# Attention with mixed heads and a PReLU layer: rows of a group 12 or 9 partitions apart, and two fixed places for side work in each block

## The chip, the cores and the metric

The kernel runs on one core of a Trainium2 chip. The metric is the device time of one execution in microseconds (us), taken as the median of several runs. Engines are named as the profile names them: PE is TensorE's matmul stream and PEld its weight loads, DVE is VectorE, ACT is ScalarE, POOL is GpSimd, SP is SyncE, which here only starts DMAs. All arithmetic on the activations of the first half is fp32.

## The reference

B = 4, H = 12 heads, S = 448, D = 64; the second half has DM = 768 and DFF = 2048.

```python
scores = q @ k.T / sqrt(D)                       # per head
scores = einsum('bhij,hg->bgij', scores, w_pre)  # heads mixed
attn = softmax(scores, axis=-1)
attn = einsum('bhij,hg->bgij', attn, w_post)     # mixed again
x = (attn @ v) laid out as (B*S, H*D)
h = x @ w_in
out = (max(h, 0) + alpha * min(h, 0)) @ w_out
```

## The kernel before, in words

The program has two halves. The first (to about 545 us) does the attention, and beside it VectorE turns the float64 weights of the second half into fp32. The second half (from about 553 us) is a stream of matmuls. The change touches the first half alone.

**Chunks and groups.** The 448 query rows of a batch are cut into chunks of 110, 110, 110 and 118 rows (L27). For a chunk and one head pair `qk` (L140) puts raw scores into a PSUM tile `s`, and ScalarE copies them into the SBUF tile `st` (L155), which holds one query row per partition, with 12 heads times 448 keys behind it. Head mixing needs the 12 heads of a row on 12 partitions. So a chunk is cut into groups of GI = 10 rows, and `relay` (L159) moves a group with one SBUF-to-SBUF DMA, from 10 partitions of `st` to the 120 partitions of a tile `sr`. There are 180 groups, 45 in a batch, and two of them make a block: 90 blocks. Each relay moves 10 x 12 pieces of 448 floats (1,792 bytes), 215,040 bytes in all. There are eight `sr` buffers, so relays run up to four blocks ahead.

**A block.** `mix` multiplies the two relayed groups by the weights into PSUM tile `m` (L170, 8 matmuls); VectorE takes the negated row maxima `nm` (L175); ScalarE takes two exponentials into `e` (L182), one for each half u; `norm` makes the scaled second mixing weights `r`; two blocks later `post` does the second mixing, transposing as it goes, into the one PSUM tile `pa` (L204, 56 matmuls), and ScalarE copies `pa` in two pieces into `at` (L214).

**Side work.** For each chunk there are six `qk` jobs (8 matmuls and one eviction by ScalarE each), and two `pv` jobs, which multiply `at` by `v` (L226, 84 matmuls) and are evicted by a ScalarE copy (L235), a VectorE addition (L236) and a DMA to the DRAM tensor `x2` (L237). The PSUM tiles of both kinds, `s` and `x`, share one buffer (`ps_s`, one tile of two banks), so that a job's matmuls wait for the eviction of the job before it.

**What sets the order.** Each engine works through its own instructions in program order, and `step(m)` writes that order: the mix of block m+1, the DMAs left over from the step before, the relays of block m+4, norm and maximum, both exponentials of block m, the first side job with its eviction, the second mixing of block m-2 with its copies, then all other side jobs with theirs. A table `jobs` says which side jobs fall into which step. Relays are issued by SP for even groups and by POOL for odd ones (the first eight by SP, ACT and POOL).

Of the kernel before, what the change touches and what calls it, by code (L numbers as in the profile page):

```python
# [14 lines left out]
ALU = mybir.AluOpType  # L15
# [7 lines left out]
GI = 10  # L23
GP = GI * H
HI = GI // 2
HP = HI * H
CHUNKS = [(0, 110), (110, 110), (220, 110), (330, 118)]  # L27
CW = 118
NCC = DM // 128
NFC = DFF // 128  # L30
NP = H // 2
NS = 4
NJ = S // 64
SR0 = 4
RAHEAD = 3
LAG = 2
# [24 lines left out]
def talking_heads_prelu(ctx: ExitStack, tc: tile.TileContext, q, k, v, w_pre, w_post, mask, w_in, w_out, alpha, out):  # L61
    nc = tc.nc
# [2 lines left out]

    groups, first = [], []
    chunk_list = [(b, c) for b in range(B) for c in range(len(CHUNKS))]
    for ci, (b, c) in enumerate(chunk_list):  # L70
        first.append(len(groups))
        cn = CHUNKS[c][1]
        for r in range(0, cn, GI):
            groups.append((ci, min(r, cn - GI)))
    NG, NC = len(groups), len(chunk_list)
    NB = NG // 2
    first.append(NG)
# [34 lines left out]
    k_t, q_t, v_t, s_t, a_t = {}, {}, {}, {}, {}  # L112
# [8 lines left out]

    def load_q(ci, dmas=None):
        b, c = chunk_list[ci]
        c0, cn = CHUNKS[c]
        q_t[ci] = qp.tile([128, NP, CW], F32, tag="q", name=f"q{ci}")
        for hf in range(2):
            dma = dmas[hf] if dmas else nc.gpsimd
            dma.dma_start(out=q_t[ci][64 * hf:64 * hf + 64, :, :cn],
                          in_=q[b, :, H * c0 + NP * hf * cn:H * c0 + NP * (hf + 1) * cn])
# [7 lines left out]
    u_t = {}  # L137

    def qk(ci, p, ps_pool=None):
        b, c = chunk_list[ci]  # L140
        cn = CHUNKS[c][1]
        ps = (ps_pool or ps_s).tile([128, 2, 512], F32, tag="m" if ps_pool else "s", name=f"s{ci}_{p}")
# [7 lines left out]
    def qk_out(ci, p, copy=nc.scalar.copy):  # L150
        cn = CHUNKS[chunk_list[ci][1]][1]
        if p == 0:
            s_t[ci] = sp.tile([CW, H, S], F32, tag="s", name=f"st{ci}")
        dst = s_t[ci].rearrange("p (t n) s -> p n t s", t=2)
        copy(dst[:cn, p], u_t.pop(("qk", ci, p))[:cn, :, :S])  # L155

    sr_t, m_t, nm_t, e_t, se_t, r_t = {}, {}, {}, {}, {}, {}

    def relay(n, dma):  # L159
        ci, r = groups[n]  # L160
        sr_t[n] = sr_b[n % NSR]
        dma.dma_start(out=sr_t[n][SR0:SR0 + GP], in_=s_t[ci][r:r + GI])  # L162

    def mix(m):

# [7 lines left out]
    def rmax(m):  # L173
        nm = sm.tile([128, 2], F32, tag="nm", name=f"nm{m}")
        nc.vector.tensor_reduce(out=nm, in_=m_t[m][:, :, :S], axis=AX.X, op=ALU.max, negate=True)  # L175
        nm_t[m] = nm

    def exp(m, u):
        if u == 0:
            e_t[m] = ep.tile([128, 2, S], F32, tag="e", name=f"e{m}")  # L180
            se_t[m] = sm.tile([128, 2], F32, tag="se", name=f"se{m}")
        nc.scalar.activation(out=e_t[m][:, u], in_=m_t[m][:, u, :S], func=AF.Exp, bias=nm_t[m][:, u:u + 1], scale=1.0,  # L182
                             accum_out=se_t[m][:, u:u + 1])
# [12 lines left out]
    def post(m):  # L196
        e, r = e_t.pop(m), r_t.pop(m)
        for u in range(2):
            for jb in range(NJ):
                s, c = divmod(jb, 2)  # L200
                for g in range(2):
                    h = slice(64 * g, 64 * g + 64)
                    dst = pa[64 * c:64 * c + 64, g, s * GP:(s + 1) * GP].rearrange("p (h i) -> p h i", h=H)
                    nc.tensor.matmul(dst[:, :, HI * u:HI * u + HI], e[h, u, 64 * jb:64 * jb + 64],  # L204
                                     r[h, u].rearrange("p (h i) -> p h i", h=H), start=True, stop=True)

    def post_out(m):
        for g in range(2):
            n = 2 * m + g
            ci, r = groups[n]  # L210
            if n == first[ci]:
                a_t[ci] = ap_.tile([128, NS, H, CW], F32, tag="a", name=f"at{ci}")
            dst = a_t[ci].rearrange("p s h i -> p (s h) i")[:, :, r:r + GI]
            nc.scalar.copy(dst, pa[:, g, :NS * GP].rearrange("p (s i) -> p s i", i=GI))  # L214

    def pv(ci, hx, ps_pool=None):
        b, c = chunk_list[ci]
        cn = CHUNKS[c][1]
        ps = (ps_pool or ps_s).tile([128, 2, 512], F32, tag="m" if ps_pool else "s", name=f"x{ci}_{hx}")
        for cl in range(3):  # L220
            for s in range(NS):
                for t in range(2):
                    h = 2 * (3 * hx + cl) + t
                    for r in range(2 if 2 * s + 1 < NJ else 1):
                        pr = slice(64 * r, 64 * r + 64)
                        nc.tensor.matmul(ps[64 * t:64 * t + 64, r, cl * CW:cl * CW + cn], v_t[b][pr, s, h * D:(h + 1) * D],  # L226
                                         a_t[ci][pr, s, h, :cn], start=(s == 0), stop=(2 * s + 2 + r >= NJ))
        u_t["pv", ci, hx] = ps

    def pv_out(ci, hx):  # L230
        b, c = chunk_list[ci]
        c0, cn = CHUNKS[c]
        xe = xep.tile([128, 3, CW], F32, tag="xe", name=f"xe{ci}_{hx}")
        src = u_t.pop(("pv", ci, hx))[:, :, :3 * CW].rearrange("p r (c i) -> p r c i", c=3)
        nc.scalar.copy(xe[:, :, :cn], src[:, 0, :, :cn])  # L235
        nc.vector.tensor_tensor(xe[:, :, :cn], src[:, 1, :, :cn], xe[:, :, :cn], ALU.add)  # L236
        later.append(lambda: nc.sync.dma_start(  # L237
            out=x2[3 * hx:3 * hx + 3, :, b * S + c0:b * S + c0 + cn].rearrange("c p i -> p c i"), in_=xe[:, :, :cn]))

# [27 lines left out]
    jobs = {}  # L267

    def at(m, f, *args):
        jobs.setdefault(m, []).append((f, args))  # L270

    for ci, (b, c) in enumerate(chunk_list):
        if ci:
            m0, m1 = first[ci - 1] // 2 - RAHEAD, first[ci] // 2 - RAHEAD - 2
            for p in range(NP):
                at(max(m0 + p * (m1 - m0) // (NP - 1), p // 2), "qk", ci, p)
        if ci >= 2:
            at(max(first[ci - 2] // 2 - 1, 0), "load", load_q, ci)
        if c == 0:
            if b:  # L280
                at(first[ci] // 2 - 15, "load", load_k, b)
            at(first[ci] // 2 + 3 if b else 1, "load", load_v, b)
        lb = (first[ci + 1] - 1) // 2
        at(lb + LAG + 1, "pv", ci, 0)
        at(lb + LAG + (3 if ci + 1 < NC else 1), "pv", ci, 1)
    conv_steps = NFC * 2 * 7

    with tc.manual_schedule():
# [24 lines left out]
        for i, w in enumerate((w_pre, w_post)):  # L313
            for p in ((SR0, 64), (0, 64))[i]:
                nc.gpsimd.dma_start(out=mask_sb[p:p + HP, i], in_=mask[:HP, :HI, :])
                nc.gpsimd.dma_start(out=wb[p:p + HP, i, :],
                                    in_=w.rearrange("(o h) g -> o h g", o=1).to_broadcast([HI, H, H]))
# [5 lines left out]
            out=wk[:, :HP].rearrange("p (i g) -> p i g", g=H), in0=mask_sb[:, 0], scalar=scale,  # L323
# [4 lines left out]
            out=wq.rearrange("p g i -> p i g"), in0=mask_sb[:, 1],  # L328
# [9 lines left out]
        def relays(upto, dmas):  # L338
            nonlocal relayed
            while relayed < min(upto, NG):  # L340
                relay(relayed, dmas[relayed % len(dmas)])
                relayed += 1

        relays(2 * (RAHEAD + 1), (nc.sync, nc.scalar, nc.gpsimd))
        done = 0
        live = lambda m: 0 <= m < NB
        EV = {"qk": (qk, qk_out), "pv": (pv, pv_out)}

        def step(m):
            nonlocal done  # L350
            todo = jobs.get(m, [])
            for f, args in todo:
                if f == "load":
                    args[0](*args[1:])
            uses = [(f, args) for f, args in todo if f != "load"]
            if live(m + 1):
                mix(m + 1)
            now, later[:] = list(later), []
            for f in now:
                f()  # L360
            if m >= 0:
                relays(2 * (m + 2 + RAHEAD) if m > 2 else first[1], (nc.sync, nc.gpsimd))
            if live(m - 1):
                norm(m - 1)
            if live(m + 1):
                rmax(m + 1)
            if live(m):
                exp(m, 0)
                exp(m, 1)
            for f, args in uses[:1]:  # L370
                EV[f][0](*args)
                EV[f][1](*args)
            if live(m - LAG):
                post(m - LAG)
                post_out(m - LAG)
            for f, args in uses[1:]:
                EV[f][0](*args)
                EV[f][1](*args)
            want = (m + 1) * conv_steps // (NB - 4)
            while done < want and done < conv_steps:  # L380
                next(conv, None)
                done += 1
# [95 lines left out]
        for u in range(NU + 1):  # L478
            b, f = divmod(u, NFC)
# [4 lines left out]
            if u < NU:  # L484
                split_w(u, 1)
                ps = l1(u)
# [44 lines left out]
```

## Time and profile before

| what | us |
|---|---|
| median of 3 runs | 1043.7 |
| lowest and highest | 1034.62, 1052.75 |
| the profiled execution | 1041.12 |
| its span | 1038.9 |
| PE busy in the span | 869.1 |
| DVE, ACT, POOL busy | 500.2, 441.6, 348.7 |

Busy shares mix two halves of the program with different limits, so the rows further down are read by stretch. Between the profiled execution and its span lie 2.2 us.

### The profile page before, as it was taken

The numbers are of one execution on the slowest core, as the hardware profiler recorded it, in microseconds if no ns is written. First come the engines' busy times: TensorE is split into PE (matmuls) and PEld (weight loads), VectorE is DVE, ScalarE is ACT, GpSimd is POOL, SyncE is SP. The second block draws the span as 40 slices with busy tenths as digits, with TensorE's granted clock in tenths as the row PEclk, the third lists the DMA queues.
The fourth block names the chain that finished last, engine by engine and source line by source line (L and its number), as shares of the span: only waits on it lengthen the run. The fifth ranks groups of instructions, "written<-read, shape, count | busy, mean of one in ns | idle before, by whom it ended". The sixth has DMA issues, their size and how long they took to land.

```text
span 1038.9 us, 26286 instructions
## 1 busy us (share of the span) xinstructions
PE 869.1 (84%) x11540; PEld 687.8 (66%) x11540; DVE 500.2 (48%) x886; ACT 441.6 (43%) x870; POOL 348.7 (34%) x305
## 2 busy tenths in 40 slices
PE   4656767867868687778666999999999999999998
PEld 2134444544535355455455999999999999999997
DVE  3454666656657376758624224632265224542222
ACT  1453666655657466648342232323233323232322
POOL 3121222222212122211004455554455454545452
PEclk9687898988889798889796999999999999999999
DMA  7698878897899977898618600020001000010001
GB/s 149 154 185 193 173 190 204 220 220 179 167 228 213 200 191 181 186 247 176 145 32 316 271 1 19 1 89 1 1 19 63 27 1 9 9 54 1 1 1 53
DMA packets 55209, 123.86 MB, mean 119 GB/s; under 512 B 21080, under 2 KB 38840, under 8 KB 54712
## 3 DMA queue, kind: packets, MB, share of 16 engines
q0 software_dynamic: 15232, 59.01, 25.7%
q1 hardware_dynamic: 38546, 60.12, 20.7%
q10 hardware_dynamic: 1318, 3.08, 1.2%
q8 instruction: 90, 1.47, 0.6%
q14 instruction: 23, 0.19, 0.1%
HBM read 59.85 MB, written 23.59 MB: 80 GB/s over the span
## 4 chain that ended last, share of the span: by engine, by line
PE 67%; DMA 16%; ACT 7%; issue 5%; DVE 4%; SPq 1%; POOL 0%; ACTq 0%; DVEq 0%; POOLq 0%
PE h L435 23%; PE acc L460 23%; DMA sr<-st 14%; PE s L147 7%; PE x L226 6%; PE m L170 4%; PE pa L204 4%; ACT st L155 3%; ACT at L214 2%; ACT e L182 1%; DMA xr<-x 1%; DMA wb<-in_w_post_dram 1%; DMA cr<-in_w_out_dram 1%; DVE xe L236 1%; DVE nm L175 1%
## 5 line engine op out<-in xcount | busy, mean ns | idle before, releaser
L435 PE MATMUL h<-xs,wi 128*128 128x448 f32 x1152 | 251.4, 371 | 12.6 <-DVE xs L425 11.3
L460 PE MATMUL acc<-g,wo 128*128 128x448 f32 x1152 | 248.2, 368 | 0.0
L435 PEld LDWEIGHTS h<-xs,wi 128*128 128x128 f32 x1152 | 218.4, 190 | 35.4 <-issue 11.5
L460 PEld LDWEIGHTS acc<-g,wo 128*128 128x128 f32 x1152 | 216.2, 188 | 21.8
L413 POOL TENSOR_TENSOR wi<-wr,wi 128x768 fp32r<-128x768 f32 x64 | 118.6, 1853 | 269.8 <-ACT wi L412 269.8
L204 PEld LDWEIGHTS pa<-r,e 64*64 64x64 f32 x5040 | 115.4, 146 | 79.6 <-issue 55.4
L175 DVE TENSOR_REDUCE nm<-m 128x2 f32<-128x896 f32 x90 | 97.9, 1088 | 135.7 <-PE m L170 135.5
L444 DVE TENSOR_SCALAR t<-h,alpha_sb 128x448 f32<-128x448 f32 x64 | 43.8, 684 | 245.7 <-PE h L435 245.7
L204 PE MATMUL pa<-r,e 64*64 64x60 f32 x5040 | 121.9, 234 | 43.6 <-issue 33.8
L170 PE MATMUL m<-sr,wk 64*64 64x448 f32 (+1 forms) x720 | 111.6, 650 | 50.4 <-DMA sr<-st 43.2
L446 ACT CAST g<-t 128x448 fp32r<-128x448 f32 x64 | 36.3, 567 | 275.2 <-DVE t L445 275.2
L162 POOL DMA_DIRECT2D sr<-st x88 | 54.2, 617 | 276.9 <-PE m L170 185.0
L147 PE MATMUL s<-k,q 64*46 64x448 f32 (+2 forms) x768 | 112.7, 640 | 39.5 <-ACT st L155 27.8
L214 ACT COPY at<-pa 128x480 f32<-128x480 f32 x180 | 93.2, 572 | 82.2 <-PE pa L204 82.0
L413 POOL TENSOR_TENSOR wo<-wr,wo 128x768 fp32r<-128x768 f32 x64 | 123.8, 1935 | 7.6 <-ACT wo L412 5.9
L182 ACT ACTIVATE e<-m,nm 128x448 f32<-128x448 f32 x180 | 113.7, 646 | 14.2 <-DVE nm L175 14.2
L226 PEld LDWEIGHTS x<-at,v 64*64 64x64 f32 x2688 | 88.2, 146 | 37.6 <-issue 20.3
L155 ACT COPY st<-s 110x896 f32<-110x896 f32 (+1 forms) x93 | 84.6, 909 | 63.0 <-PE s L147 55.6
L226 PE MATMUL x<-at,v 64*64 64x110 f32 (+1 forms) x2688 | 92.6, 280 | 18.5 <-issue 13.3
L147 PEld LDWEIGHTS s<-k,q 64*64 64x64 f32 (+2 forms) x768 | 27.5, 140 | 92.3 <-ACT st L155 70.9
L170 PEld LDWEIGHTS m<-sr,wk 64*64 64x64 f32 (+1 forms) x720 | 29.3, 151 | 77.5 <-issue 64.7
L412 ACT CAST wo<-wr 128x768 fp32r<-128x768 f32 x64 | 53.8, 841 | 62.3 <-PE acc L460 62.3
(46 smaller groups left out, 564.1 us busy)
## 6 DMA issues: line engine op xcount, KB each, us to landing
sr<-st SPq DMA_DIRECT2D x89, 210.0 KB
sr<-st POOLq DMA_DIRECT2D x88, 210.0 KB, 9.7
cr<-in_w_in_dram POOLq DMA_DIRECT2D x16, 768.0 KB, 11.5
cr<-in_w_out_dram POOLq DMA_DIRECT2D x16, 768.0 KB, 10.1
wsc<-ct SPq DMA_DIRECT2D x32, 384.0 KB
wr<-wsc SPq DMA_DIRECT2D x14, 768.0 KB
xr<-x SPq DMA_DIRECT2D x24, 224.0 KB
out_dram<-o SPq DMA_DIRECT2D x24, 224.0 KB
```

The lines of the kernel that those rows point to most:

```text
L147: nc.tensor.matmul(ps[lo:hi, hf, :S], q_t[ci][r, p, lo:hi], k_t[b][r, p, :], start=True, stop=True)
L155: copy(dst[:cn, p], u_t.pop(("qk", ci, p))[:cn, :, :S])
L162: dma.dma_start(out=sr_t[n][SR0:SR0 + GP], in_=s_t[ci][r:r + GI])
L170: nc.tensor.matmul(ps[hf:hf + 64, u, :S], wk[r, :], g[r, :], start=True, stop=True)
L175: nc.vector.tensor_reduce(out=nm, in_=m_t[m][:, :, :S], axis=AX.X, op=ALU.max, negate=True)
L182: nc.scalar.activation(out=e_t[m][:, u], in_=m_t[m][:, u, :S], func=AF.Exp, bias=nm_t[m][:, u:u + 1], scale=1.0, accum_out=se_t[m][:, u:u ...
L204: nc.tensor.matmul(dst[:, :, HI * u:HI * u + HI], e[h, u, 64 * jb:64 * jb + 64], r[h, u].rearrange("p (h i) -> p h i", h=H), start=True, s ...
L214: nc.scalar.copy(dst, pa[:, g, :NS * GP].rearrange("p (s i) -> p s i", i=GI))
L226: nc.tensor.matmul(ps[64 * t:64 * t + 64, r, cl * CW:cl * CW + cn], v_t[b][pr, s, h * D:(h + 1) * D], a_t[ci][pr, s, h, :cn], start=(s == ...
L413: nc.gpsimd.tensor_tensor(t[:, 1], w, t[:, 0], ALU.subtract)
L435: nc.tensor.matmul(ps[:, :S], w[:, tw, cc * 128:(cc + 1) * 128], x[:, tx, cc, :], start=(i == 0), stop=(i == 3 * NCC - 1))
L460: nc.tensor.matmul(accs[c][:, :S], w[:, tw, c * 128:(c + 1) * 128], g[:, tg], start=(f == 0 and i == 0), stop=(f == NFC - 1 and i == 2))
```

## The change

Chunks become 120, 120, 120 and 97 rows. A new table ROWS gives for each chunk the first row used and the distance between the rows of a group: a group of a 120-row chunk is rows r, r+12, ..., r+108, and there are 12 such groups; in the last chunk a group is rows 7+r, 16+r, ..., 88+r, nine groups that use 90 of its 97 rows (two rows of the sequence are computed twice). The relay thus reads ten partitions 12 or 9 apart where it read ten neighbours; its pieces, its destination and its bytes are the same, and there are still 180 groups and 90 blocks. Since a group's rows are no longer neighbours, `at` keeps groups one behind the other, and the eviction of `pv` puts rows back into order by writing `xe` with a step of 12 or 9 floats.

In `step`, the second mixing now stands ahead of the side jobs, and there are at most two of those in a step. The first one's eviction comes after the copies of the second mixing. The second one's eviction is held over to the next step, where it stands between the two exponentials. Relays are issued behind that held eviction. A new table places the jobs.

```diff
-CHUNKS = [(0, 110), (110, 110), (220, 110), (330, 118)]
-CW = 118
+CHUNKS = [(0, 120), (120, 120), (240, 120), (351, 97)]
+ROWS = [(0, 12), (0, 12), (0, 12), (7, 9)]
+CW = 120
...
-        cn = CHUNKS[c][1]
-        for r in range(0, cn, GI):
-            groups.append((ci, min(r, cn - GI)))
+        for r in range(ROWS[c][1]):
+            groups.append((ci, r))
...
-        dma.dma_start(out=sr_t[n][SR0:SR0 + GP], in_=s_t[ci][r:r + GI])
+        r0, st = ROWS[chunk_list[ci][1]]
+        r0 += r
+        dma.dma_start(out=sr_t[n][SR0:SR0 + GP], in_=s_t[ci][r0:r0 + (GI - 1) * st + 1:st])
...
-            dst = a_t[ci].rearrange("p s h i -> p (s h) i")[:, :, r:r + GI]
+            dst = a_t[ci].rearrange("p s h i -> p (s h) i")[:, :, r * GI:(r + 1) * GI]
...
-        src = u_t.pop(("pv", ci, hx))[:, :, :3 * CW].rearrange("p r (c i) -> p r c i", c=3)
-        nc.scalar.copy(xe[:, :, :cn], src[:, 0, :, :cn])
-        nc.vector.tensor_tensor(xe[:, :, :cn], src[:, 1, :, :cn], xe[:, :, :cn], ALU.add)
+        ps = u_t.pop(("pv", ci, hx))[:, :, :3 * CW].rearrange("p r (c i) -> p r c i", c=3)
+        src = [ps[:, r, :, :cn].rearrange("p c (g i) -> p c g i", i=GI) for r in range(2)]
+        dst = xe[:, :, :cn].rearrange("p c (i g) -> p c g i", i=GI)
+        nc.scalar.copy(dst, src[0])
+        nc.vector.tensor_tensor(dst, src[1], dst, ALU.add)
...
-            uses = [(f, args) for f, args in todo if f != "load"]
+            uses = sorted(((f, args) for f, args in todo if f != "load"), key=lambda u: u[0] != "pv")
             if live(m + 1):
                 mix(m + 1)
...
-            if m >= 0:
-                relays(2 * (m + 2 + RAHEAD) if m > 2 else first[1], (nc.sync, nc.gpsimd))
+            if live(m - LAG):
+                post(m - LAG)
             if live(m - 1):
                 norm(m - 1)
             if live(m + 1):
                 rmax(m + 1)
             if live(m):
                 exp(m, 0)
+            for f, args in held:
+                EV[f][1](*args)
+            if m >= 0:
+                relays(2 * (m + 2 + RAHEAD) if m > 2 else first[1], (nc.sync, nc.gpsimd))
+            if live(m):
                 exp(m, 1)
             for f, args in uses[:1]:
                 EV[f][0](*args)
+            if live(m - LAG):
+                post_out(m - LAG)
+            for f, args in uses[:1]:
                 EV[f][1](*args)
-            if live(m - LAG):
-                post(m - LAG)
-                post_out(m - LAG)
             for f, args in uses[1:]:
                 EV[f][0](*args)
-                EV[f][1](*args)
+            held[:] = uses[1:]
```

The planner that fills `jobs` is rewritten too; what it makes is this. With x for a `pv` job and s for a `qk` job, the 94 steps of before are 21 with no job, 34 with s, 5 with x, 7 with s s, 12 with x s, 13 with x s s, one with four s and one with x x. Those of the change are 16 with none, 27 with s, 7 with x, 20 with s s, 23 with x s and one with x x.

On PE the matmuls of block 26's mix up to the last job of step 27 stand like this before (m is a mix, pa a second mixing, x3 the two `pv` jobs of chunk 3, s6 the `qk` jobs of chunk 6):

```order
L170 MATMUL m26_1984<-sr5_115,wk_108 64x448 x2
L226 MATMUL x3_0_2003<-at3_1523,v0_276 64x118 x42
L204 MATMUL pa_118<-r23_1935,e23_1882 64x12x5 x28
L147 MATMUL s6_0_2079<-k1_627,q6_1700 64x448 x2
L147 MATMUL s6_0_2079<-k1_627,q6_1700 46x448 x2
L147 MATMUL s6_1_2086<-k1_627,q6_1700 64x448 x2
L147 MATMUL s6_1_2086<-k1_627,q6_1700 46x448 x2
L170 MATMUL m27_2094<-sr6_116,wk_108 64x448 x2
L170 MATMUL m27_2094<-sr7_117,wk_108 64x448 x2
L147 MATMUL s6_2_2113<-k1_627,q6_1700 64x448 x2
L147 MATMUL s6_2_2113<-k1_627,q6_1700 46x448 x2
L204 MATMUL pa_118<-r24_1995,e24_1939 64x12x5 x28
```

and with the change like this:

```order
L173 MATMUL m26_1984<-sr5_115,wk_108 64x448 x2
L207 MATMUL pa_118<-r23_1961,e23_1907 64x12x5 x28
L229 MATMUL x3_0_2031<-at3_1685,v0_288 64x90 x42
L148 MATMUL s6_0_2079<-k1_621,q6_1698 64x448 x2
L148 MATMUL s6_0_2079<-k1_621,q6_1698 56x448 x2
L173 MATMUL m27_2086<-sr6_116,wk_108 64x448 x2
L173 MATMUL m27_2086<-sr7_117,wk_108 64x448 x2
L207 MATMUL pa_118<-r24_2021,e24_1965 64x12x5 x28
L148 MATMUL s6_1_2135<-k1_621,q6_1698 64x448 x2
L148 MATMUL s6_1_2135<-k1_621,q6_1698 56x448 x2
L148 MATMUL s6_2_2143<-k1_621,q6_1698 64x448 x2
L148 MATMUL s6_2_2143<-k1_621,q6_1698 56x448 x2
```

The second mixing stood between the first side job and the others; now it stands ahead of both, and the two side jobs, which share one PSUM buffer, follow each other directly.

On ACT the same steps (e is a pair of exponentials or one of them, xe and st are evictions of side jobs, at the copies of the second mixing) stand like this before:

```order
L235 COPY xe3_0_2046<-x3_0_2003 128x354
L214 COPY at4_1972<-pa_118 128x48x10 x2
L155 COPY st6_2084<-s6_0_2079 110x2x448
L155 COPY st6_2084<-s6_1_2086 110x2x448
L182 ACTIVATE e26_2109,se26_2110<-m26_1984,nm26_1997 128x448 x2
L155 COPY st6_2084<-s6_2_2113 110x2x448
L214 COPY at4_1972<-pa_118 128x48x10 x2
```

and with the change like this:

```order
L217 COPY at4_1972<-pa_118 128x48x10 x2
L242 COPY xe3_0_2076<-x3_0_2031 128x3x9x10
L185 ACTIVATE e26_2127,se26_2128<-m26_1984,nm26_2023 128x448
L156 COPY st6_2130<-s6_0_2079 120x2x448
L185 ACTIVATE e26_2127,se26_2128<-m26_1984,nm26_2023 128x448
L217 COPY at4_1972<-pa_118 128x48x10 x2
L156 COPY st6_2130<-s6_1_2135 120x2x448
L185 ACTIVATE e27_2194,se27_2195<-m27_2086,nm27_2125 128x448
L156 COPY st6_2130<-s6_2_2143 120x2x448
L185 ACTIVATE e27_2194,se27_2195<-m27_2086,nm27_2125 128x448
```

A first job's eviction has moved behind the copies of the second mixing, and a second job's to between the exponentials of the next step.

## Rows read from the trace of the kernel before

**Rows 1.** The page's head and its picture of the span in 40 slices of 26 us: busy tenths of PE, the clock granted to TensorE in tenths, and the mean busy share of the 16 DMA engines in tenths.

```profile
span 1038.9 us, 26286 instructions
...
PE   4656767867868687778666999999999999999998
...
PEclk9687898988889798889796999999999999999999
DMA  7698878897899977898618600020001000010001
```

**Rows 2.** Stretches of the span: from and to, length, busy us (instructions) of PE, PEld, DVE, ACT and POOL, granted clock, DMA share, GB/s.

```profile
60.00:120.00 60.00, 39.13 (x894) 26.50 (x898) 31.55 (x63) 28.57 (x65) 10.02 (x17) 0.83 0.88 190
...
240.00:300.00 60.00, 47.04 (x1255) 31.71 (x1248) 41.21 (x84) 39.79 (x89) 13.61 (x23) 0.93 0.84 186
300.00:360.00 60.00, 41.85 (x985) 26.88 (x989) 33.66 (x69) 30.70 (x68) 11.92 (x20) 0.83 0.98 217
...
553.00:1039.00 486.00, 479.43 (x2304) 434.65 (x2304) 183.45 (x252) 140.31 (x201) 239.48 (x127) 0.99 0.12 45
...
345.00:350.00 5.00, 4.22 (x24) 1.42 (x28) 0.86 (x1) 2.87 (x6) 0.60 (x1) 0.50 1.05 207
351.00:358.00 7.00, 5.32 (x166) 3.77 (x157) 3.70 (x9) 4.09 (x9) 0.60 (x1) 1.00 1.05 212
...
27.00:543.00 516.00, 377.86 (x9168) 246.35 (x9168) 307.65 (x615) 294.42 (x661) 96.54 (x157) 0.86 0.80 185
```

**Rows 3.** The chain that ended last, cut to 18 to 545 us: its shares by line, and of its pieces (start us, us, what) the first and the last of the nine longest waits for relays.

```profile
by line: DMA sr<-st 26.9%; PE s L147 12.6%; PE x L226 11.2%; issue 10.4%; PE m L170 8.7%; PE pa L204 8.0%; ACT st L155 6.6%; ACT at L214 3.7%; ACT e L182 2.8%; DMA cr<-in_w_out_dram 1.3%; DVE xe L236 1.3%; DVE nm L175 1.2%; ACT xe L235 1.0%
...
18.41 15.33 DMA sr<-st
...
482.92 14.36 DMA sr<-st
```

**Rows 4.** What PE waited for between 20 and 545 us: engine, line <- releaser, us in total, times, the longest.

```profile
PE m L170 <- DMA sr<-st: 43.2, 11, 9.7
PE pa L204 <- issue: 33.8, 14, 6.2
PE s L147 <- ACT st L155: 27.8, 34, 3.2
PE x L226 <- issue: 13.3, 6, 4.9
PE pa L204 <- ACT at L214: 9.5, 14, 1.1
PE m L170 <- issue: 6.2, 2, 3.8
```

**Rows 5.** DMA queues (packets, MB, share of 16 engines' time) and issues between 20 and 553 us. q0 is POOL's, q1 that of SP, q8 carries instructions. One issue is one DMA, with KB each and median us to landing.

```profile
q0 software_dynamic: 14654, 57.76, 49.0%
q1 hardware_dynamic: 29325, 37.80, 28.8%
...
q8 instruction: 72, 1.18, 1.0%
...
sr<-st SPq DMA_DIRECT2D x87, 210.0 KB
sr<-st POOLq DMA_DIRECT2D x86, 210.0 KB, 9.2
```

**Rows 6.** The queues of the same view between 553 and 1039 us.

```profile
q1 hardware_dynamic: 8561, 21.42, 11.9%
q8 instruction: 18, 0.29, 0.2%
```

**Rows 7.** All POOL relays of the span, from issue to landing (view of tile sr).

```profile
DMA to landing us min/median/max: 5.3/9.7/21.7
```

**Rows 8.** Instructions in order of time: start us, us, engine, line, operation, output<-input, tile, count, and in brackets the idle time before it and what ended it. The two rows before 350 us lie behind a stop of PE, the others in the stretch after it, and the last one shows the next stop.

```profile
345.78 1.76 PE L147 MATMUL s<-k,q 64*64 64x448 f32 x8 [1.03 <-ACT st L155]
...
347.33 1.71 PE L170 MATMUL m<-sr,wk 64*64 64x448 f32 x8
...
350.31 1.12 PE L204 MATMUL pa<-r,e 64*64 64x60 f32 x56
...
350.58 0.91 ACT L155 COPY st<-s 118x896 f32<-118x896 f32 x1 [0.82 <-PE s L147]
...
351.48 1.03 ACT L214 COPY at<-pa 128x480 f32<-128x480 f32 x2
...
351.55 0.97 PE L147 MATMUL s<-k,q 64*64 64x448 f32 x8
...
352.35 0.93 PE L170 MATMUL m<-sr,wk 64*64 64x448 f32 x8
...
353.40 0.64 ACT L182 ACTIVATE e<-m,nm 128x448 f32<-128x448 f32 x1
...
353.56 2.38 PE L226 MATMUL x<-at,v 64*64 64x110 f32 x81 [0.28 <-ACT st L155]
...
354.54 0.21 ACT L182 ACTIVATION_READ_ACCUMULATOR e<-m,nm 128x1 f32 x1
...
356.08 0.43 ACT L235 COPY xe<-x 128x330 f32<-128x330 f32 x1 [1.34 <-PE x L226]
356.55 0.50 DVE L236 TENSOR_TENSOR xe<-x,xe 128x330 f32<-128x330 f32 x1 [2.08 <-ACT xe L235]
...
359.84 0.40 PE L204 MATMUL pa<-r,e 64*64 64x60 f32 x13 [3.12 <-issue]
```

More of the change, by code (lines that the diff above doesn't have):

```diff
@@ L123, in load_q @@
         b, c = chunk_list[ci]
-        c0, cn = CHUNKS[c]
+        c0, cn = sum(n for _, n in CHUNKS[:c]), CHUNKS[c][1]
         q_t[ci] = qp.tile([128, NP, CW], F32, tag="q", name=f"q{ci}")
@@ L217, in pv @@
         b, c = chunk_list[ci]
-        cn = CHUNKS[c][1]
+        cn = ROWS[c][1] * GI
         ps = (ps_pool or ps_s).tile([128, 2, 512], F32, tag="m" if ps_pool else "s", name=f"x{ci}_{hx}")
@@ L231, in pv_out @@
         b, c = chunk_list[ci]
-        c0, cn = CHUNKS[c]
+        r0, st = ROWS[c]
+        c0, cn = CHUNKS[c][0] + r0, st * GI
         xe = xep.tile([128, 3, CW], F32, tag="xe", name=f"xe{ci}_{hx}")
-        src = u_t.pop(("pv", ci, hx))[:, :, :3 * CW].rearrange("p r (c i) -> p r c i", c=3)
-        nc.scalar.copy(xe[:, :, :cn], src[:, 0, :, :cn])
-        nc.vector.tensor_tensor(xe[:, :, :cn], src[:, 1, :, :cn], xe[:, :, :cn], ALU.add)
+        ps = u_t.pop(("pv", ci, hx))[:, :, :3 * CW].rearrange("p r (c i) -> p r c i", c=3)
[3 more added lines that the diff above has]
+        nc.vector.tensor_tensor(dst, src[1], dst, ALU.add)
         later.append(lambda: nc.sync.dma_start(
@@ L270, in at, with laid_out @@
         jobs.setdefault(m, []).append((f, args))
+    def laid_out(n):
+        return max(n // 2 - RAHEAD - 1, 0 if n < first[1] else 3)
+    for ci in range(NC):
+        lb = (first[ci + 1] - 1) // 2
+        at(lb + LAG + 1, "pv", ci, 0)
+        at(lb + LAG + (3 if ci + 1 < NC else 1), "pv", ci, 1)
     for ci, (b, c) in enumerate(chunk_list):
         if ci:
-            m0, m1 = first[ci - 1] // 2 - RAHEAD, first[ci] // 2 - RAHEAD - 2
-            for p in range(NP):
-                at(max(m0 + p * (m1 - m0) // (NP - 1), p // 2), "qk", ci, p)
+            m1 = laid_out(first[ci]) - 1
+            m0 = laid_out(first[ci - 1]) + 1 if ci > 1 else -1
+            free = lambda m: 2 - len(jobs.get(m, []))
+            room = [(m, 0) for m in range(m0, m1 + 1) if free(m)]
+            room += [(m, 1) for m in range(m0, m1 + 1) if free(m) == 2]
+            room += [(m0 - 1, i) for i in range(free(m0 - 1))]
+            for p, (m, _) in enumerate(sorted(room[:NP])):
+                at(m, "qk", ci, p)
+            assert len(room) >= NP
+    for ci, (b, c) in enumerate(chunk_list):
         if ci >= 2:
@@ L282, in talking_heads_prelu @@
             at(first[ci] // 2 + 3 if b else 1, "load", load_v, b)
-        lb = (first[ci + 1] - 1) // 2
-        at(lb + LAG + 1, "pv", ci, 0)
-        at(lb + LAG + (3 if ci + 1 < NC else 1), "pv", ci, 1)
     conv_steps = NFC * 2 * 7
@@ L347, in talking_heads_prelu @@
         EV = {"qk": (qk, qk_out), "pv": (pv, pv_out)}
+        held = []
         def step(m):
```

## The prediction

> **What bounds the kernel now.** I read the picture of the span first [rows 1], then stretches, the chain of waits, PE's waits and the DMA queues. The second half, 553 to 1039 us, is PE at 479 busy of 486 us at a clock of 0.99, with DMA engines busy 0.12 of the time [rows 2]: nothing in the change reaches it. The first half is different: PE is busy 42 to 47 of 60 us, ACT and DVE less, and the DMA engines 0.80 of 516 us, up to 0.98 [rows 2]. The chain says what this costs: between 18 and 545 us relays hold 26.9% of it, in waits of up to 26 us of which the first and last are shown, and "issue" 10.4% [rows 3]. Those are not yet savings, since PE works on other things beside most of them. What PE itself lost is in its waits: 43.2 us for relays, 53.3 us for issue (33.8 + 13.3 + 6.2), 37.3 us for ACT's evictions (27.8 + 9.5) [rows 4].
>
> "Issue" names no engine. In this half PE goes through four times the instructions of the other (9,168 matmuls to 2,304 [rows 2]), and queue q8 brings 72 instruction packets of 16 KB (1.18 MB / 72) in 20 to 553 us, 18 in the second half [rows 5, 6]. Stops of 3 us in the middle of one run of matmuls [rows 8] fit a fetch that came late. So I take issue as waits for instructions, behind the same busy DMA engines.
>
> [...]
>
> **What a relay costs.** In 20 to 553 us q0 and q1 moved 95.6 MB in 49.0% + 28.8% of 16 engines' 533 us, that is 6,635 engine-us [rows 5]. 173 relays of 215,040 bytes are 37.2 MB of it, in 173 x 120 = 20,760 pieces. In the second half q1 moved 21.42 MB in 11.9% of 16 x 486 us = 925 engine-us, or 23.2 GB/s per engine [rows 6]. If everything but relays ran at that rate, 58.4 MB would take 2,517 engine-us; 4,118 are left, 198 ns a piece of 1,792 bytes, against 77 ns at 23.2 GB/s. These are the ends for a relay's piece after the change: 198 ns (distance between the rows does nothing) and 77 ns (it costs what other traffic costs). I take 77, because the pieces, their size, their destination and the issuing queues are the same and the ten source partitions are the one thing left that other transfers do not have.
>
> [...]
>
> **The change part by part.**
> - *DMA load.* 20,760 pieces x 121 ns = 2,512 engine-us less, 6,635 to 4,123, or 258 us on each of 16 engines, in a phase of some 450 us: 0.57 busy instead of 0.80.
> - *Waits for relays, 43.2 us.* A relay lands 9.7 us after issue in the median, 21.7 at worst and 5.3 at best [rows 7], and is issued three blocks ahead of its mix: 13 us and more. Near the best value none is late but the first. Ends 0 and -43; I take -38, leaving 5 for the start.
> - *Waits for instructions, 53.3 us.* Ends 0 (fetches are slow for their own reasons) and -53. A fetch queues behind relay pieces, so I scale with a piece: 53.3 x 77 / 198 = 21 stay, -32.
> - *Clock.* PE's warm work in the half is 90 blocks x (0.95 mix + 1.12 second mixing), 96 `qk` x 0.97 and 32 `pv` x 2.4 [rows 8]: 187 + 93 + 77 = 357 us, against 378 busy [rows 2]. The 21 us too many follow the stops; 70 of 96 us of stops go, so -15. Ends 0 and -21.
> - *The new order.* Now the second mixing stands ahead of both side jobs, which share one PSUM buffer. In a step s s the first s ends 0.97 us after the second mixing; ACT then still has copies (1.03) and the eviction (0.91) to do [rows 8], so the second s waits 1.0 us. In x s it waits for the x eviction, 0.43 + 0.50 and hand-over [rows 8], 1.05 us. That is 43 steps and 44 us; steps with one s or none are set by ACT (copies 1.03, exponentials 1.35 from first start to last end, eviction 0.91 [rows 8]) at 3.3 and 2.4 us against PE's 3.05 and 2.08, another 11 us. 55 us in all where 37 stand now [rows 4]: +18. Counted the same way the old order gives 31 (13 steps x s s and the step of four s lose 16, the rest 15), so the ends are 0, if second jobs find their evictions done, and +24.
> - *Queues.* Relays stand behind a held eviction in program order, but only a chunk's first relays read what it writes; SP and POOL issue the same DMAs in nearly the same order, with stores of `x2` and weights ahead of relays as before. Nothing is charged; if SP came to wait for a late `xe`, the relay behind it would eat into its three blocks first.
> - *Same count, same price.* Evictions of 120 or 97 rows are as long as of 110, since the 896 columns set them; `qk` still has 768 matmuls; `pv` has the same matmuls on 120 and 90 columns, 450 for 448 in a batch. Two rows more per batch cost nothing.
> - *Strided `xe`.* The writes step 48 or 36 bytes. No row shows such a write. Between unchanged and doubled lie 0 and 32 x (0.43 + 0.50) = +30 us; I take 0, since the copies of `at`, which also write in broken runs (of 40 bytes), cost 0.52 us for 480 elements against 0.43 for 330 [rows 8]. [...]
>
> **Sum.** 1041.1 (the profiled execution) - 38 - 32 - 15 + 18 = 974 us. That execution is 2.6 us under the median of 1043.7, and by runs between 1034.6 and 1052.8 about 2%, 21 us, is what this kernel's measurement tells from no change.
>
> **Rivals.**
> 1. *Instruction waits stay.* Packets of q8 took 1.0% of 16 x 533 us / 72 = 1.2 us each in the first half and 0.2% of 16 x 486 us / 18 = 0.9 us in the second [rows 5, 6]: hardly slower, which speaks against their being held up by relays on the engines. Then 1041.1 - 38 - 8 + 18 = 1013.
> 2. *All stops go and the order is free.* 1041.1 - 43 - 53 - 21 = 924. For it: ACT's waits of 37 us now are partly an echo of stops. Against it: the shared buffer.
> 3. *The distance does nothing, and the order breaks even.* Relay pieces are slow for another reason (only ten at a time, on both sides in SBUF), DMA share stays at 0.80: 1041. For it: nothing in this trace shows two distances side by side.
> 4. *Slower.* Relays stay as slow, and the second place in a step costs its wait: the second side job of 43 steps stands idle behind ACT's copies, and since PE's stops for DMA come at other moments they hide none of it. 1041.1 + 24 = 1065, and 1080 with half the strided-write bound. It decides once pieces stay near 200 ns and PE's waits for evictions go over 60 us. Against it: the relays share the chain with nothing else that large.
>
> **Numbers.** Forecast (950 to 1000) 0.44; rival 1, up to 1025, 0.21; rival 2 (920 to 950) 0.14; rival 3 0.13; rival 4 0.08. The prediction is 974 us. From 922 to 1022 us lie the forecast, nearly all of rivals 1 and 2: 0.78, and the bounds at both ends. Faster by over 2% (under 1023): 0.44 + 0.14 + 0.19 = 0.77; within 2%: 0.13 + 0.02 = 0.15; slower: 0.08.
>
> **What would show it.** Right: POOL's relays land in some 5 us, the DMA share of the first half falls to about 0.6, q0 and q1 together to some 4,100 engine-us; "DMA sr" all but leaves PE's waits, issue falls to about 20 us; PE's wait for evictions rises to about 55 us with `s` and `x` as its lines; the first half ends near 480 us. Wrong: landing times as before (rivals 3, 4); landing quick but issue still at 50 us (rival 1); an ACT or DVE busy over 0.9 of the stretch, which I exclude by their 294 and 308 of 516 us [rows 2]; an eviction at `xe` of twice its time.

## The result, and the profile after

The changed kernel takes 998.6 us in the median against 1042.1 us: a ratio of 0.957, 95% interval 0.944 to 0.970. That is faster, inside the range, and 25 us short of the gain that was forecast (43 of 67 us). Medians are of all runs of a kernel; ratios are to the kernel before on the same chip, without the slow runs of either, and since the second half, which no change below reaches, takes about 484 us in some executions and about 494 in others, single profiles are compared by where the attention ends.

The profiled execution took 1008.9 us, 10 above the median; a second profile of the same kernel (e1_same below, 985.5 us) stands beside it where it matters. First the two halves of the changed kernel's span, with the columns of [rows 2].

```profile
0.00:515.00 515.00, 370.66 (x9236) 242.40 (x9236) 322.62 (x634) 304.94 (x667) 107.55 (x178) 0.90 0.71 197
515.00:1007.00 492.00, 480.87 (x2304) 435.27 (x2304) 183.22 (x252) 141.88 (x203) 240.19 (x128) 0.99 0.13 46
```

The second half is what it was, within 3 us (from the first load of `x2` on, at 545.3 us before and 510.4 now). The first ended 35 us earlier, at a granted clock of 0.90, with DMA engines busy 0.71 of it: less than before, more than the 0.57 expected. What PE waited for between 20 and 515 us, to be read against [rows 4]:

```profile
PE s L148 <- DVE xe L243: 37.6, 23, 1.7
PE m L173 <- DMA sr<-st: 29.5, 5, 8.8
PE s L148 <- ACT st L156: 28.2, 23, 4.4
PE m L173 <- ACT e L185: 9.7, 11, 2.0
PE x L229 <- issue: 9.4, 5, 3.1
PE pa L207 <- issue: 4.4, 4, 2.1
```

Waits for instructions have fallen from 53 to 14.5 us (with 0.7 on L148), those for relays from 43 to 29.5. On top is a line that stood at 2.5 us before: `s` waits 23 times for the addition into `xe`, once in each step x s. The mix now also waits for exponentials, 9.7 us. For ACT and DVE together PE waits 89 us where it waited 48 (all such lines of the view, those not shown too). The DMA queues in the same stretch, against [rows 5]:

```profile
q0 software_dynamic: 14424, 57.68, 44.2%
q1 hardware_dynamic: 28710, 36.85, 24.3%
...
sr<-st POOLq DMA_DIRECT2D x86, 210.0 KB, 7.2
```

68.5% of 16 x 495 us is 5,425 engine-us. By the prediction's balance (all but 174 relays at 23.2 GB/s) a relay's piece costs 142 ns, between the two ends of 198 and 77.

The times of the single packets in the traces say more. Relays are the packets of 1,792 bytes on q1 and those of 5,376 bytes, three pieces, on q0. From 20 us to the end of the attention a piece of them took 153 ns before and 99 now, and everything else on these two queues ran at 16.9 GB/s per engine, before and now. So the balance, with 23.2 GB/s for the rest, puts the relay's price 43 to 45 ns too high on both sides; the fall, 54 to 56 ns, is the same either way.

And the evictions of v's products (view of tile x; times are min/median/max in ns), against 0.43 and 0.50 us for 330 floats in [rows 8]:

```profile
L242 ACT COPY xe<-x x32: 636/778/796, 73.0 to 507.7; 128x360 f32<-128x360 f32 x24, 128x270 f32<-128x270 f32 x8
L243 DVE TENSOR_TENSOR xe<-x,xe x32: 635/780/808, 73.8 to 508.3; 128x360 f32<-128x360 f32 x24, 128x270 f32<-128x270 f32 x8
```

### The profile page after: what moved, and what is told of

Its sections match the earlier page's. It is cut to its first block, busy times and chain, and to the rows that moved or that the text cites. A ratio compares the mean times of both kernels' runs of the same rounds, so it can differ in the third digit from the quotient of the medians.

```text
span 1006.9 us, 26281 instructions
## 1 busy us (share of the span) xinstructions
PE 851.5 (85%) x11540; PEld 677.7 (67%) x11540; DVE 505.8 (50%) x886; ACT 446.8 (44%) x870; POOL 347.7 (35%) x305
## 3 DMA queue, kind: packets, MB, share of 16 engines
q0 software_dynamic: 15008, 59.09, 22.3%
## 4 chain that ended last, share of the span: by engine, by line
PE 71%; DMA 10%; ACT 8%; DVE 6%; issue 4%; POOL 1%; SPq 0%; ACTq 0%; DVEq 0%; POOLq 0%
PE acc L489 24%; PE h L464 23%; DMA sr<-st 8%; PE x L229 7%; PE s L148 6%; PE pa L207 6%; PE m L173 5%; ACT st L156 3%; ACT e L185 2%; ACT xe L242 2%; ACT at L217 2%; DVE xe L243 2%; DMA xr<-x 1%; DVE nm L178 1%; DMA wb<-in_w_post_dram 1%
## 5 line engine op out<-in xcount | busy, mean ns | idle before, releaser
L464 PE MATMUL h<-xs,wi 128*128 128x448 f32 x1152 | 252.8, 372 | 14.5 <-DVE xs L454 13.0
L148 PE MATMUL s<-k,q 64*64 64x448 f32 (+2 forms) x768 | 109.2, 607 | 68.9 <-DVE xe L243 37.6
L173 PE MATMUL m<-sr,wk 64*64 64x448 f32 (+1 forms) x720 | 101.7, 622 | 43.9 <-DMA sr<-st 29.5
L207 PE MATMUL pa<-r,e 64*64 64x60 f32 x5040 | 114.7, 235 | 10.6 <-issue 4.4
L156 ACT COPY st<-s 120x896 f32<-120x896 f32 (+1 forms) x93 | 85.2, 916 | 74.7 <-PE s L148 66.3
L229 PE MATMUL x<-at,v 64*64 64x120 f32 (+1 forms) x2688 | 89.9, 272 | 12.3 <-issue 9.4
L148 PEld LDWEIGHTS s<-k,q 64*64 64x64 f32 (+2 forms) x768 | 24.2, 136 | 101.3 <-ACT st L156 47.2
L229 PEld LDWEIGHTS x<-at,v 64*64 64x64 f32 x2688 | 81.8, 140 | 14.0 <-issue 10.5
```

The costliest lines, as they stand in the source:

```text
L148: nc.tensor.matmul(ps[lo:hi, hf, :S], q_t[ci][r, p, lo:hi], k_t[b][r, p, :], start=True, stop=True)
L173: nc.tensor.matmul(ps[hf:hf + 64, u, :S], wk[r, :], g[r, :], start=True, stop=True)
L464: nc.tensor.matmul(ps[:, :S], w[:, tw, cc * 128:(cc + 1) * 128], x[:, tx, cc, :], start=(i == 0), stop=(i == 3 * NCC - 1))
```

## The experiments

Times are compared as ratios to the kernel before, run on the same chip with each set of four; 0.01 is 10 us. "A piece" is worked out by the balance above, each from its own profile's first half; "by its packets" is the mean time of the packets themselves.

**The same kernel again.**

> The changed kernel again, unaltered, so that the others are compared with it on the same chip and so that there is a second profile of it. Every theory expects 0.957 of the kernel before, 990 to 1005 us. Its profile should show again PE waiting some 70 to 90 us for evictions and 30 us or less for relays and for instructions each; if the three long stops for relays lie elsewhere or are gone, they belong to one execution and not to the kernel.

988.2 us in the median, 2 us under the expected range, ratio 0.956 (0.947 to 0.965). PE's waits in its profile:

```profile
PE s L148 <- DVE xe L243: 37.8, 23, 1.7
PE s L148 <- ACT st L156: 30.2, 23, 5.9
PE m L173 <- DMA sr<-st: 22.3, 7, 6.0
PE x L229 <- issue: 12.8, 7, 3.3
...
PE m L173 <- ACT e L185: 11.0, 11, 3.7
PE pa L207 <- issue: 9.0, 7, 3.5
```

The picture repeats: 22 us for relays, 23 for instructions in all, 88 for ACT and DVE (all such lines of the view up to the second half); a piece costs 141 ns, 99 by its packets. The chain's three long waits for relays come again, at 41, 177 and 273 us. The shape belongs to the kernel, the split between its DMA lines to the execution. Busy time in its attention, with the columns of [rows 2]:

```profile
20.00:498.00 478.00, 345.90 (x9168) 229.56 (x9168) 314.08 (x616) 300.73 (x662) 96.02 (x157) 0.92 0.72 201
```

**Neighbouring rows in the new order.**

```diff
-        r0 += r
-        ... in_=s_t[ci][r0:r0 + (GI - 1) * st + 1:st])
+        r0 += r * GI
+        ... in_=s_t[ci][r0:r0 + GI])
```

> The changed kernel with the relays reading ten neighbouring rows again; everything else, the strided writes of xe too, is as in the change, so the rows of a chunk come out in another order. Theory (the distance makes relays fast): POOL relays land in 9 to 10 us instead of 7, a relay piece is back near 200 ns, PE's waits for relays and instructions go from some 45 us back to 80 to 100 us, and the time to 1040 to 1060 us, no better than the kernel before. Rival (the gain comes from the order of the steps, and the distance does nothing): 990 to 1005 us, landing times as in the changed kernel.

1037.4 us, ratio 0.993 (0.984 to 1.003): no gain is left; the expected range began at 1040. A POOL relay's landing (view of tile sr):

```profile
DMA to landing us min/median/max: 5.2/9.6/20.0
```

PE's waits for relays and instructions in the same kernel:

```profile
PE m L173 <- DMA sr<-st: 36.3, 5, 13.7
...
PE x L229 <- issue: 27.7, 10, 6.0
PE pa L207 <- issue: 13.3, 11, 2.3
PE s L148 <- issue: 4.7, 2, 2.7
```

and its two DMA queues from 20 to 515 us:

```profile
q0 software_dynamic: 14367, 57.55, 49.7%
q1 hardware_dynamic: 26324, 35.04, 29.7%
```

Relays land as in [rows 7], a piece is back at 189 ns (150 by its packets), and relays and instructions are waited for 83 us, 38 more than in the run before. With nothing altered but which ten partitions are read, this settles where the gain comes from, and that in one and the same order the waits for instructions grow with the price of a relay too.

Against the kernel before, this one has the new order, the chunks of 120 rows and the strided write, and takes no longer. Their waits do not vanish: PE waits 89 us for ACT and DVE, as with spaced rows and 41 more than before. They are paid for by 13.5 us less of waiting for relays and instructions and by 19 us less of PE's busy time (359.0 us at a granted clock of 0.89, against 377.9 at 0.86). Which of the three brings that was not told apart.

**The old order with spaced rows.** `step` and the job table are those of the kernel before, the rest is the change.

> The rows spaced as in the change, with the steps and the table of jobs of the kernel before (second mixing behind the first side job, every eviction in its own step, relays ahead of the maximum). Theory (distance brings the gain, the new order costs waits for evictions): PE's waits for evictions fall from some 85 us to 40 to 55 us, relays and instruction waits stay as in the change, 960 to 985 us. Rival (the order brings the gain): 1030 to 1045 us, with instruction waits back near 50 us.

979.5 us in the median; its four runs, 959.8 to 983.5 us, scatter too widely for an interval. The time is the theory's; the waits for evictions, 61 us, are over its 40 to 55. PE's waits:

```profile
PE s L148 <- ACT st L156: 28.8, 37, 9.7
PE pa L207 <- issue: 20.5, 9, 6.5
PE m L173 <- DMA sr<-st: 18.1, 4, 6.9
PE x L229 <- issue: 15.1, 7, 5.1
PE s L148 <- DVE xe L243: 12.2, 17, 0.9
```

Waits for ACT and DVE fall from 88 to 61 us in all, while those for instructions rise from 23 to 39, so the two do not simply add. That a stop of PE for an eviction is time in which instructions catch up would explain it; it was not tested.

**Evictions in one run.**

```diff
-        dst = xe[:, :, :cn].rearrange("p c (i g) -> p c g i", i=GI)
+        dst = xe[:, :, :cn].rearrange("p c (g i) -> p c g i", i=GI)
```

> The changed kernel with the two evictions of v's products writing xe in one run instead of with a step of 12 or 9 floats; the rows come out in another order, nothing else differs. The copy and the addition should go from 0.78 us each to 0.45 and 0.52. Theory (they stand on the path, because the second side job waits for them in 23 steps): 23 x 0.6 = 14 us less, 980 to 988 us. Rival (they are hidden): within 3 us of the changed kernel.

975.9 us, under the 980 to 988 expected, ratio 0.945 (0.936 to 0.953), 0.011 or 11.5 us less than the same kernel again. The two intervals overlap, and by the two profiles the attention ends only 4 us earlier, so the size rests on the evictions and on the waits for them. The evictions' medians are 459 and 533 ns:

```profile
L242 ACT COPY xe<-x x32: 385/459/460, 73.2 to 492.8; 128x360 f32<-128x360 f32 x24, 128x270 f32<-128x270 f32 x8
L243 DVE TENSOR_TENSOR xe<-x,xe x32: 429/533/533, 73.7 to 493.2; 128x360 f32<-128x360 f32 x24, 128x270 f32<-128x270 f32 x8
```

and `s` waits 25.3 instead of 37.8 us for `xe` in the 23 steps. 23 x (0.32 + 0.25) = 13 us is what the step costs in these waits, and all waits for ACT and DVE fall from 88 to 73.

**Reading PSUM with the step instead, in the old order.**

```diff
-        src = [ps[:, r, :, :cn].rearrange("p c (g i) -> p c g i", i=GI) for r in range(2)]
-        dst = xe[:, :, :cn].rearrange("p c (i g) -> p c g i", i=GI)
+        src = [ps[:, r, :, :cn].rearrange("p c (g i) -> p c i g", i=GI) for r in range(2)]
+        dst = xe[:, :, :cn].rearrange("p c (i g) -> p c i g", i=GI)
```

> Rows spaced as in the change, order of the kernel before, and v's products put back into row order by reading PSUM with a step of 10 floats and writing xe in one run, where the change reads in one run and writes with a step of 12. Theory (the step costs where SBUF is written, not where PSUM is read): the copy 0.44 to 0.50 us and the addition 0.50 to 0.55 instead of 0.75 each, and 8 to 15 us less than the 979 us of the old order with spaced rows: 964 to 972 us. Rival (a step costs on either side): 0.7 us and more each, 975 to 985 us.

965.7 us, ratio 0.921 (0.913 to 0.929): the quickest so far. The same 459 and 532 ns as without any step:

```profile
L242 ACT COPY xe<-x x32: 385/459/460, 75.2 to 477.4; 128x360 f32<-128x360 f32 x24, 128x270 f32<-128x270 f32 x8
L243 DVE TENSOR_TENSOR xe<-x,xe x32: 426/532/534, 75.7 to 477.8; 128x360 f32<-128x360 f32 x24, 128x270 f32<-128x270 f32 x8
```

This kernel differs from the one before it (straight `xe`, new order) by the order alone, as far as prices go. By the ratios, 0.945 to 0.921, whose intervals do not meet, the new order costs 25 us; by the medians of all runs it is 10, and by the two profiles 15 us of the attention's end (493.2 to 477.8 us in the rows above). Two other pairs give less. Old order with spaced rows against the same kernel again: 9 us by medians, 3 by the attention's end. The last experiment against k in parts: 13 us by ratios, of which the strided write has 11.5. So every pair says that the order costs time, but the size, 2 to 25 us, is not settled.

**k in parts.** In the changed kernel's chain the three longest pieces are relays (start us, us):

```profile
43.71 22.11 DMA sr<-st
...
180.19 14.91 DMA sr<-st
...
283.44 28.33 DMA sr<-st
```

and POOL issues the next batch's k in each of them or just ahead (same kernel, POOL's instructions in order of time):

```profile
48.64 0.54 POOL L120 DMA_DIRECT2D k<-in_k_dram  x1
...
179.68 1.25 POOL L120 DMA_DIRECT2D k<-in_k_dram  x2
...
294.57 1.06 POOL L120 DMA_DIRECT2D k<-in_k_dram  x2
```

```diff
-                at(first[ci] // 2 - 15, "load", load_k, b)
+                for p in range(NP):
+                    at(first[ci] // 2 - 15 + p, "load", load_k_part, b, p)
```

> The changed kernel with each later batch's k loaded in six parts of 224 KB, one in each of six steps, in pieces of 1,792 bytes, instead of two loads of 336 KB in one step, in pieces of 10,752 bytes. Theory (the relay waits that are left are relays caught beside a burst of k in large pieces): the long waits of the chain next to k loads go, PE's wait for relays falls from 22 to 30 us to under 14, and the time by 10 to 20 us against the same kernel with whole loads, to 970 to 980 us. Rival (it is the bytes, or the relays of a chunk's beginning themselves): same relay waits, 985 to 1000 us.

980.3 us, ratio 0.934 (0.922 to 0.946) against 0.956 (0.947 to 0.965) of the changed kernel. PE waits 14.5 us for relays instead of 22 to 30, so that both figures of the theory are just missed; by its view of waits:

```profile
PE m L180 <- DMA sr<-st: 14.5, 5, 5.8
```

and the longest relay of POOL lands after 15.4 instead of 19 to 21 us (view of tile sr):

```profile
DMA to landing us min/median/max: 2.4/6.9/15.4
```

The waits fell, but not where the theory says: the chain's long pieces at 42 and 271 us stayed, 17 and 18 us long, where the same kernel again, with whole loads, has 16 and 16. In that profile, moreover, the piece at 273 us is all but over when k is issued, at 288.6. So it is not shown that k's burst makes the waits that are left, and of bytes at once, size of the pieces and a relay's place behind the load in POOL's queue none was told from the others.

**Relays without the weights' traffic.** The conversion of the weights is moved behind the attention, once with spaced and once with neighbouring rows (one run each).

> The changed kernel with the conversion of the weights moved whole behind the attention, so that the relays share the DMA engines with q, k, v and x2 alone; its total time (some 150 us more) says nothing, its first half is what is read. Theory (distance sets a relay's price): POOL relays land in 3 to 5 us, a relay piece takes 70 to 110 ns of an engine, no wait for relays apart from k loads.

> As the run before with the relays reading ten neighbouring rows (rows of a chunk come out in another order). Theory (distance sets a relay's price, whatever else is on the engines): POOL relays land in 6 to 9 us and a piece takes 180 to 260 ns of an engine, twice the spaced rows or more. Rival (relays are slow because of the weights' traffic beside them): landing and price within a fifth of the spaced rows.

From issue to landing, spaced:

```profile
DMA to landing us min/median/max: 2.5/4.5/15.1
```

and neighbours:

```profile
DMA to landing us min/median/max: 5.0/7.9/19.5
```

The queue rows of the two, spaced rows from 20 to 460 us and neighbours from 20 to 520:

```profile
q0 software_dynamic: 10070, 34.03, 30.1%
q1 hardware_dynamic: 23543, 24.35, 19.5%
```

```profile
q0 software_dynamic: 10138, 34.19, 37.1%
q1 hardware_dynamic: 23570, 24.40, 25.4%
```

A piece costs 124 ns spaced and 196 as neighbours, or 101 and 172 by its packets. So the price of neighbours is the relay's own: it is no lower without the weights than with them, 189 to 198 (150 to 153 by packets). "Twice or more" was wrong, it is 1.6 to 1.7 times, and the 70 to 110 ns are met by the packets alone. The lower end of the prediction, 77 ns, is not reached even here. PE still waits 6.0 us for relays. The quickest relay lands in half the time, 2.5 against 5.0 us, and the attention's last store is issued at 462.7 us with spaced rows and at 525.3 with neighbours.

**Rows 4, 2 and 8 apart.** The groups of the 120-row chunks take other rows:

```diff
+        if st == 12:
+            r0, st = 40 * (r // 4) + r % 4, 4
...
+            r0, st = 20 * (r // 2) + r % 2, 2
...
+            r0, st = (r, 8) if r < 8 else (72 + r, 4)
```

> The changed kernel with the groups of the 120-row chunks made of rows 4 apart (rows 0, 4, ..., 36 and so on in three blocks of 40) instead of 12; the last chunk keeps 9; the rows of a chunk come out in another order. [...] Rival (distance as such): a third of the way from 1 to 12 at best, 170 to 185 ns, 1015 to 1035 us.

> As the run before with rows 2 apart in blocks of 20. [...] Rival (distance as such): as the neighbours, 185 ns and more, 1030 to 1045 us.

> As the runs before with eight of the twelve groups of rows 8 apart and the other four of rows 4 apart. [...] Rival (distance as such): better than 4 apart, close to 12 apart.

| rows apart | a piece, ns | by its packets, ns | POOL's landing, median us | us, median | ratio (interval) |
|---|---|---|---|---|---|
| 1 | 189 | 150 | 9.6 | 1037.4 | 0.993 (0.984 to 1.003) |
| 2 | 159 | 121 | 8.7 | 1012.6 | 0.977 (0.970 to 0.983) |
| 8 and 4 | 153 | 111 | 8.2 | 999.0 | none |
| 4 | 148 | 107 | 8.1 | 1004.4 | 0.971 (0.964 to 0.977) |
| 12 and 9 | 141 | 99 | 7.7 | 988.2 | 0.956 (0.947 to 0.965) |

The queue rows behind these prices, from 20 to 500 us of each kernel's DMA view, for 2 apart:

```profile
q0 software_dynamic: 14480, 57.85, 48.0%
q1 hardware_dynamic: 27234, 36.22, 27.6%
```

for 8 and 4 apart:

```profile
q0 software_dynamic: 14424, 57.68, 46.9%
q1 hardware_dynamic: 28032, 36.59, 26.6%
```

and for 4 apart:

```profile
q0 software_dynamic: 14420, 57.70, 46.6%
q1 hardware_dynamic: 27225, 36.20, 25.4%
```

Two rows apart already brings nearly half of the gain, which distance as such would not by its forecast (4 apart should then have been 1015 us or more, and was 1004; 2 apart 1030 or more, and was 1013). Nor are 8 and 4 apart better than 4 apart, as distance would have it: a piece costs 153 against 148 ns, or 111 against 107 by its packets. Their median time is 5 us lower than that of 4 apart, without an interval.

Taken in the order of the relays in each queue, the packets can be told apart by group. Their mean price in ns by place in a 120-row chunk (the eight relays of the start left out):

| groups of a chunk | neighbours | 2 apart | 8 and 4 apart | 4 apart | 12 apart |
|---|---|---|---|---|---|
| first four | 155 | 143 | 131 | 121 | 105 |
| middle four | 145 | 116 | 109 | 99 | 102 |
| last four | 154 | 124 | 107 | 110 | 94 |

In the kernel of 8 and 4 apart the first and the middle groups are of rows 8 apart, and there they cost some 10 ns more than those of 4 apart (131 against 121, 109 against 99); the last groups read the same rows in both kernels and are level within the errors (107 against 110). So the price is not set by distance alone. It also changes with the place: in the kernel of 4 apart the middle groups (rows 40 to 79) cost 99 ns, near the 102 of 12 apart, and the first (rows 0 to 39) 121; in all but the kernel of 12 apart the first groups cost 10 to 27 ns more than the middle ones. What sets the price was not shown. This rests on one profile of each kernel, with standard errors of 3 to 8 ns, and in the whole program's time 4 apart and 8 and 4 apart do not separate.

**All together.** Old order, PSUM read with a step, k in parts.

> Rows spaced as in the change, the steps of the kernel before, v's products put in order by reading PSUM, and k loaded in six parts. Theory (what the runs so far gained adds up): 966 us less about 8, 952 to 965 us, with PE's wait for relays under 14 us. Rival (the k parts gave nothing of their own): 966 us again.

963.9 us, ratio 0.921 (0.912 to 0.931): in the theory's range, but the same as without the k parts, as the rival says. PE's waits:

```profile
PE pa L214 <- issue: 20.4, 11, 4.5
PE s L155 <- ACT st L163: 19.9, 36, 1.7
PE x L236 <- issue: 17.4, 8, 5.7
PE m L180 <- DMA sr<-st: 13.5, 4, 5.9
```

Relay waits fell from 19.6 to 13.5 us, instruction waits rose from 36 to 45 (all such lines): here the gain went into the next wait, and waits for instructions are now the largest.

## Why the prediction came out as it did

The time lies inside the range, and faster relays are the cause, as forecast. Most of the signs that the prediction named for being right did not come: relays of POOL land in 7.1 to 7.7 us and not in 5, the DMA share is 0.71 and not 0.6, relays are still waited for, evictions cost far more than 55 us, and the attention ends at 499 to 510 us and not at 480. Only the waits for instructions are as foretold. What PE waits and what it is busy add up to the stretch from 20 us to the attention's end, so the terms can be set beside the profile of the same kernel again:

| term | forecast, us | measured, us |
|---|---|---|
| waits for relays | -38 | -21 (43.2 to 22.3) |
| waits for instructions | -32 | -31 (53.3 to 22.7) |
| PE busy, by the clock | -15 | -32 (377.9 to 345.9) |
| waits for ACT and DVE | +18 | +40 (48.1 to 87.7) |
| sum | -67 | -44 |

The changed kernel's first profile has -14, -39, -21 and +41. The last term is steady, the first three move from one execution to the next. That the first and the third nearly make up for each other is luck; what is missing of the gain is the fourth.

- **Faster relays: right in kind, the price of a piece wrong.** The step that failed is the 77 ns, taken "because the ten source partitions are the one thing left". It came to 137 to 142 ns by the prediction's own balance. That balance failed too: it lets everything else run at the 23.2 GB/s of the second half, and in the first it ran at 16.9. By its packets a piece went from 153 to 99 ns, under half of the fall that was forecast. So relays land later than forecast, and 22 to 30 us of waits for them stay where 5 were expected.
- **Clock: more than its upper end.** PE ran the same 9,168 matmuls at a granted clock of 0.92 instead of 0.86, with 7 stops of over 3 us instead of 18. Its 345.9 us are less than the 357 that the prediction worked out for the full clock, so that sum was too high. That the 21 us between 357 and 378 follow PE's stops, from which the -15 was taken, no run shows; [rows 2, 8] have one stretch at a clock of 0.50 behind a stop.
- **Waits for instructions: right in size.** With neighbours they are 47 us, with spaced rows 23, in the same order, and rival 1, that they stay, is out for this change. That "issue" is a wait for instructions, which the prediction inferred, the traces bear out: each of the 17 such stops of over 1 us before, and of the 8 in the same kernel again, ends 1.1 to 1.7 us after an instruction packet of q8 has ended. That a fetch queues behind relay pieces, from which the -32 was scaled, no run shows, and why packets come late stays open: they took 1.15 us each before and 1.14 to 1.16 after, and with fast relays in the old order the waits are 36 to 45 us.
- **The new order, +18: right in kind, 5 us too small in waits** (50 us for ACT and DVE in the old order with the read from PSUM, 73 in the new one with `xe` in one run). The two places where the wait was put, 23 steps x s and 20 steps s s, are where it stands: `s` waits for `xe` 23 times and for `st` 23 times. In time it cost 2 to 25 us, since other waits fell. Evictions into `st` do cost the same whatever their rows: 0.91 us for 120 and 0.92 for 97 (L156, first profile), against 0.91 for 110 and for 118 before (L155).
- **The strided write, 0: wrong, 12 to 14 us of waits, 11.5 us by ratios.** The failed step is the row chosen for it: the copies of `at` write runs of ten floats, the write of `xe` single floats, and is not like them. It took 0.78 us where 0.46 and 0.53 stand without the step. By the runs the step costs 0.32 and 0.25 us for 360 floats a partition (e1_same against e4_straight_xe); why it does was not shown.
- **Rivals 3 and 4** (the distance does nothing) fall with the run on neighbouring rows. Both conditions of rival 4, pieces near 200 ns and over 60 us of waits for evictions, are met there, and still the time is that of the kernel before, 0.993 and not 1065 us.

## What to carry to other kernels

Where a DMA out of SBUF reads few partitions, try which ones it reads: ten rows 12 or 9 apart instead of ten neighbours halved the landing time of the quickest transfers (2.5 against 5.0 us without the weights' traffic) with the same bytes and pieces, and took 4% off the program in the new order and 7 to 8% in the old one (there together with the chunks of 120 rows). If that scrambles an order that must be restored, restore it in the read from PSUM, where the step was free here (459 and 532 ns, as without it), and not in the write to SBUF (778 and 780 ns). And before a step's order is rewritten along with such a change, time the two apart: with neighbouring rows the new order and the strided write cost no time, with spaced rows both did.

## What was not expected of the hardware

ACT and DVE read PSUM with a step of 10 floats at the speed of an unbroken read (459 and 532 ns for 360 floats), but take 778 and 780 ns where `xe` in SBUF has a step of 12 (ACT only writes it, DVE's addition reads it too). And PE's waits for instructions follow the price of a relay in one order (47 and 23 us, or 44 and 25 without the weights' traffic), but not the share of time that the DMA engines are busy: they are 23 us at a share of 0.72 and 25 at 0.51.
